# Sliding-window attention followed by a feed-forward pair: loads per pair, a new order of the transfers, first value casts on ScalarE, attention steps spread through the feed-forward, groups of 384 tokens

## The chip, the cores and the metric

One core of a Trainium2 chip. The metric is the device time of one execution in microseconds (us), the median over several runs. Two kernels that are compared ran on the same chip, in turns. A ratio is the mean time of one kernel's fast runs over that of the other's fast runs of the same rounds, so it is not quite the ratio of the medians that are quoted.

The engines are TensorE (PE, with PEld for its weight loads), VectorE (DVE), ScalarE (ACT), GpSimd (POOL) and SyncE (SP), which here only issues DMAs. The clock that the traces record for PE is either full (1.0) or half (0.5).

A line of a timeline reads: start and duration in us, engine, line of the kernel, operation, output<-inputs, shapes, how many instructions are merged in the line; in brackets the idle time in us just before it and what ended it.

## The reference, cut to what matters

```python
# q, k, v: (8 batches, 8 heads, 576 positions, 64); window 32
scores = q @ k.T / 8, masked to |i - j| <= 32
attn = softmax(scores);  x = attn @ v           # reshaped to (4608 tokens, 512)
h = x @ w_in                                     # 512 -> 2048
out = np.maximum(0.01 * h, h) @ w_out            # 2048 -> 512, float32
```

## The kernel before

Attention is cut into 64 steps: 8 batches, 2 halves of 288 queries, 4 pairs of heads. A step scores one pair against its window (`score`), takes exp on ACT, multiplies by a mask on POOL, and then sums and weights the values on PE (`weighted`); DVE takes the reciprocal of the sums and writes the result into `xT`.

```python
def score(i):
    ...  # 5 matmuls into ps (one buffer)
    nc.scalar.activation(out=e, in_=ps[...], func=AF.Exp, scale=scale)
    nc.gpsimd.tensor_mul(pr, e, mask[hf])

def weighted(i):
    ...  # 2 matmuls with ones into s, 5 with vbd into x (one buffer each)
    nc.vector.reciprocal(r, s)
    nc.vector.tensor_mul(xT[:, p, t0:t0 + HALF], x, r)

def step():                      # i = next step
    step_transposes(...)         # of the next batch's q and k, on PE
    score(i + 1)
    weighted(i)
    ...                          # casts of the next batch (POOL), loads of the one after (SP)
```

The feed-forward works on groups of tokens: `h_tile` (4 matmuls, then a leaky ReLU on ACT) and `o_tile` (16 matmuls, a copy on DVE into one of two `o_sb` buffers, a DMA out). All engines run in program order, so where a step stands between the tiles decides what PE can do while the chain of the step runs. The start of the kernel:

```python
for i in range(NPAIR):                       # steps 0 to 3
    score(i + 1)
    if i + 1 < NPAIR:
        cast_v(0, i + 1)                     # POOL
    load_w_in(512 * i, 512 * i + 512)        # issued by POOL
    weighted(i)
...
load_after(1, w_in_bf[0:1, 0, 1024:1026])    # q, k of batch 1, behind the third quarter of w_in
load_v(1, 0, NPAIR)
...  # h of 512 tokens, with steps 4 to 7
...  # w_out issued after the casts of batch 1
for p in range(NPAIR):                       # steps 8 to 11
    if p + 1 < NPAIR:
        cast_v(1, p + 1)
    step()
load_after(2, ...); load_v(2, 0, NPAIR)      # whole loads of batch 2
o_tile(0, 0); o_tile(0, 1); step(); o_tile(256, 0); step(); o_tile(256, 1)

groups = [(512 + 256 * i, 256) for i in range(3)]
groups += [(1280 + 512 * i, 512) for i in range(6)] + [(1280 + 512 * 6, 256)]
...  # chunks: 16 to 32 h matmuls or one o_tile each; before each, as many steps as its deadline asks
```

The softmax here doesn't subtract the row's maximum and nothing guards it: scores larger than these inputs give would overflow.

## Time and profile before

| | before |
|---|---|
| median (4 runs, those of the later comparison) | 389.96 us |
| span of the profiled run | 386.2 us |
| PE busy | 338.7 us (88%) |
| mean granted clock of PE | 0.958 |
| DVE, ACT, POOL busy | 56%, 44%, 47% |
| dense matmul work, worked out in the prediction | 310.9 us |

The row to read is the difference between the span and the dense work: 75.3 us in which PE either waits or runs at half clock. The prediction below shows the lines that this rests on.

### The profile page before, as it was taken

How to read it: one execution, taken by the hardware profiler on the slowest of the kernel's cores; microseconds unless marked ns; L12 is line 12 of the kernel's file. 1: busy time of each engine (PE TensorE's matmuls, PEld its weight loads, DVE VectorE, ACT ScalarE, POOL GpSimd, SP SyncE). 2: the span in 40 equal slices, each digit the busy share in tenths (PEclk: the TensorE clock that was granted, in tenths of full speed). 3: DMA queues.
4: the chain of work that ended last, by engine and by line, in shares of the span. 5: the costliest groups of instructions: out<-in, count | busy, mean ns of one | idle time of the engine just before them, and what ended most of it. 6: DMA issues, size and time to landing. Idle time of an engine off the chain costs nothing.

```text
span 386.2 us, 6261 instructions
## 1 busy us (share of the span) xinstructions
PE 338.7 (88%) x2496; PEld 201.9 (52%) x2496; DVE 215.2 (56%) x242; ACT 171.8 (44%) x325; POOL 182.4 (47%) x216
## 2 busy tenths in 40 slices
PE   2549775984699799999999997999799989999995
PEld 2337563443577567455555554555455545544472
DVE  4575838319567776137866757574748575600201
ACT  5716481023556537373276244723563255045060
POOL 7596798065655756025566528363735332100000
PEclk9999896897899999999999998999989999999999
DMA  8979996994946590920737290929101100110101
GB/s 193 173 111 167 239 185 110 247 171 143 229 52 168 133 145 36 225 76 27 126 80 209 94 176 0 230 72 139 40 0 39 71 2 1 56 54 0 73 38 54
DMA packets 60004, 42.34 MB, mean 110 GB/s; under 512 B 38984, under 2 KB 55368, under 8 KB 59976
## 3 DMA queue, kind: packets, MB, share of 16 engines
q1 hardware_dynamic: 55688, 37.76, 46.0%
q0 software_dynamic: 4288, 4.20, 7.2%
q8 instruction: 19, 0.31, 0.4%
q14 instruction: 9, 0.07, 0.1%
HBM read 36.70 MB, written 9.44 MB: 119 GB/s over the span
## 4 chain that ended last, share of the span: by engine, by line
PE 68%; DVE 3%; ACT 1%; issue 1%; POOL 1%; DVEq 0%; POOLq 0%
PE mm L266 29%; PE mm L257 29%; PE x L239 3%; PE ps L213 3%; PE tp L180 3%; DVE r L245 2%; PE s L231 1%; PE s L232 1%; ACT e L219 1%; DVE xT L247 0%; POOL pr L223 0%; POOL qb L161 0%; DVE o_sb L271 0%; ACT kT L194 0%; DVEq L247 0%
## 5 line engine op out<-in xcount | busy, mean ns | idle before, releaser
L223 POOL TENSOR_TENSOR pr<-e,mask 128x544 bf16<-128x544 bf16 x64 | 77.5, 1212 | 138.4 <-ACT e L219 127.9
L257 PE MATMUL mm<-xT,w_in_bf 128*128 128x256 bf16 (+1 forms) x768 | 138.5, 338 | 2.4 <-DVE xT L247 2.4
L245 DVE RECIPROCAL r<-s 128x288 f32<-128x288 f32 x64 | 125.2, 1957 | 21.8 <-PE s L232 20.7
L261 ACT ACTIVATE gT<-mm 128x256 bf16<-128x256 f32 (+1 forms) x192 | 93.8, 491 | 87.0 <-PE mm L257 82.9
L266 PE MATMUL mm<-w_out_bf,gT 128*128 128x512 bf16 x576 | 130.5, 383 | 0.0
L257 PEld LDWEIGHTS <-w_in_bf 128*128 128x128 bf16 x768 | 76.9, 102 | 53.2 <-issue 6.2
L266 PEld LDWEIGHTS <-gT 128*128 128x128 bf16 x576 | 55.8, 99 | 63.6 <-issue 2.5
L271 DVE COPY o_sb<-mm 128x512 f32<-128x512 f32 x36 | 24.9, 691 | 82.1 <-PE mm L266 72.4
L197 DVE COPY kbd<-kT 64x576 bf16<-64x576 bf16 x64 | 28.6, 447 | 53.3 <-ACT kT L194 52.8
L219 ACT ACTIVATE e<-ps 128x544 bf16<-128x544 f32 x64 | 39.9, 624 | 26.3 <-PE ps L213 26.2
L168 POOL CAST vbd<-vf 64x576 bf16<-64x576 f32 x64 | 42.3, 660 | 2.1 <-DMA vf<-in_v_dram 0.2
L194 ACT ACTIVATE kT<-tp 128x576 bf16<-128x576 bf16 x32 | 20.8, 649 | 49.3 <-PE tp L180 48.3
L188 ACT ACTIVATE qT<-tp 128x576 bf16<-128x576 bf16 x32 | 20.7, 648 | 40.5 <-PE tp L180 40.4
L231 PE MATMUL s<-pr,ones_bd 128*128 128x288 bf16 x64 | 19.8, 309 | 19.2 <-DVE r L245 13.3
L247 DVE TENSOR_TENSOR xT<-x,r 128x288 bf16<-128x288 f32 x64 | 29.3, 458 | 6.7
L239 PE MATMUL x<-pr,vbd 128*128 128x128 bf16 (+2 forms) x320 | 28.4, 225 | 3.1 <-POOL vbd L168 2.2
L213 PE MATMUL ps<-qT,kbd 128*128 128x128 bf16 (+2 forms) x320 | 28.4, 224 | 2.1 <-ACT e L219 1.8
L161 POOL CAST kb<-kf 96x768 bf16<-96x768 f32 x32 | 26.5, 828 | 7.6 <-DMA kf<-in_k_dram 7.6
L239 PEld LDWEIGHTS <-vbd 128*128 128x128 bf16 x320 | 22.3, 104 | 9.2 <-POOL vbd L168 3.7
L180 PE MATMUL tp<-ident,qb 96*128 96x96 bf16 x192 | 15.1, 221 | 11.8 <-DVE qb L161 6.7
L213 PEld LDWEIGHTS <-kbd 128*128 128x128 bf16 x320 | 20.1, 105 | 4.3 <-issue 2.7
L180 PEld LDWEIGHTS <-qb 96*128 96x128 bf16 x192 | 12.6, 106 | 17.1 <-DVE qb L161 9.3
(30 smaller groups left out, 114.4 us busy)
## 6 DMA issues: line engine op xcount, KB each, us to landing
qf<-in_q_dram SPq DMA_DIRECT2D x32, 288.0 KB, 4.3
kf<-in_k_dram SPq DMA_DIRECT2D x32, 288.0 KB, 7.1
out_dram<-o_sb SPq DMA_DIRECT2D x36, 256.0 KB, 2.1
vf<-in_v_dram SPq DMA_DIRECT2D x14, 576.0 KB, 11.2
w_in_bf<-in_moe_w_in_dram POOLq DMA_DIRECT2D x8, 256.0 KB, 4.7
w_out_bf<-in_moe_w_out_dram POOLq DMA_DIRECT2D x4, 512.0 KB, 12.0
vf<-in_v_dram SPq DMA_DIRECT2D x4, 144.0 KB, 6.9
vf<-in_v_dram SPq DMA_DIRECT2D x2, 288.0 KB, 9.2
```

Source lines behind the costliest of these rows:

```text
L168: nc.gpsimd.tensor_copy(out=vbd[b % 2][r, p, :, r], in_=vf[b][r, p])
L180: nc.tensor.transpose(tp[:, c], src[:, p, c].rearrange("p a d -> p (a d)"), ident[0:96, 0:96],)
L197: nc.vector.tensor_copy(out=kbd[b % 2][r, p, :, r], in_=kT[r].rearrange("p (n j) -> p n j", j=64),)
L213: nc.tensor.matmul(ps[:, c0:c0 + n], kbd[b % 2][:, p, blk], qT[b][:, p, q0:q0 + n], start=True, stop=True,)
L219: nc.scalar.activation(out=e, in_=ps[:, 512 - HALF:512 - HALF + NCOL], func=AF.Exp, scale=scale,)
L223: nc.gpsimd.tensor_mul(pr, e, mask[hf])
L239: nc.tensor.matmul(x[:, a:a + n], vbd[b % 2][:, p, blk, :], pr[:, c0:c0 + n], start=(n_ == 0), stop=(n_ == len(WIN[hf]) - 1), skip_group_c ...
L245: nc.vector.reciprocal(r, s)
L247: nc.vector.tensor_mul(xT[:, p, t0:t0 + HALF], x, r)
L257: nc.tensor.matmul(h[:, 0:n], w_in_bf[:, c, ts(f, 128)], xT[:, c, ds(t0, n)], start=(c == 0), stop=(c == DMC - 1),)
L261: nc.scalar.activation(out=gT[t0][:, f, 0:n], in_=h[:, 0:n], func=AF.Prelu, alpha=0.01)
L266: nc.tensor.matmul(o, gT[t0][:, f, ts(j, 128)], w_out_bf[:, f, :], start=(f == 0), stop=(f == FFC - 1),)
```

## The change

Its intent: have every transfer and cast of the start ready earlier, never let attention steps stand alone on PE, and make the deadlines of the steps gentler. The diff, cut to its core:

```diff
-    def load_qk(b, p0, p1): ...     # one tile for all pairs
+    def load_qk(b, p, behind=None): # one tile per pair; `behind` makes it wait for other data
 ...
-            nc.gpsimd.tensor_copy(out=vbd[b % 2][r, p, :, r], in_=vf[b][r, p])
+            if on_act:
+                nc.scalar.activation(out=vbd[...], in_=vf[b, p][r], func=AF.Copy)
+            else:
+                nc.gpsimd.tensor_copy(out=vbd[...], in_=vf[b, p][r])
 ...
-            step_transposes(8 * (b + 1) + PLAN[b > 1][0][r])
+            step_transposes(max(upto - 1, 8 * (b + 1)))
         score(i + 1); weighted(i)
+            step_transposes(upto)    # the last one follows the step
+        # each load follows the cast of its own pair
 ...
     score(0)
+    load_w_in(0, 512)
     first_pair(); ...; cast_qk(0, 3, nc.vector)
+    load_w_in(512, 1024)
     for i in range(NPAIR):
         score(i + 1)
-            cast_v(0, i + 1)
-        load_w_in(512 * i, 512 * i + 512)
+            cast_v(0, i + 1, on_act=True)
+        if i < 2: load_w_in(1024 + 512 * i, 1536 + 512 * i)
+        else: load_w_out(i - 2)
         weighted(i)
 ...
+    # q, k of batch 1 behind the second quarter of w_in; step 4; the rest of w_out
+    # steps 5 to 7 inside the first h group; v of batch 1 behind the second quarter of w_out
 ...
-    for p in range(NPAIR): (cast_v); step()          # steps 8 to 11, then 4 o_tiles with 2 steps
+    for p in range(NPAIR):
+        if p < 3:
+            cast_v(1, p); (at p == 2 also cast_v(1, 3))
+            o_tile(256 * (p // 2), p % 2, step if p == 2 else None)   # one step midway
+            step()
+        else:
+            o_tile(256, 1)
+        load_qk(2, p)
+    for p in range(NPAIR): load_v(2, p)
 ...
-    groups += [(1280 + 512 * i, 512) for i in range(6)] + [...]
+    groups += [(1280 + 384 * i, 384) for i in range(8)] + [...]
-    LEAD, RATE = 2, 1.2
+    RATE = 1.3                       # lead 1 for the first 12 chunks, then 2
```

## The prediction

> **What bounds the kernel now.** I read the page's busy row first, then its slices, then the same core cut into stages, then TensorE's timeline.
>
> ```profile
> span 386.2 us, 6261 instructions
> PE 338.7 (88%) x2496; PEld 201.9 (52%) x2496; DVE 215.2 (56%) x242; ACT 171.8 (44%) x325; POOL 182.4 (47%) x216
> ...
> PEclk9999896897899999999999998999989999999999
> DMA  8979996994946590920737290929101100110101
> ```
>
> TensorE (PE) is the bound: nothing else exceeds 56%. But busy is not full speed: the granted clock falls to 0.6 to 0.8 in some early slices, and the first slices are not full either. The stage table (columns: PE, weight loads, DVE, ACT, POOL busy, clock, DMA share, GB/s) shows where:
>
> ```profile
> 0.00:28.00 28.00, 12.14 (x101) 8.24 (x102) 16.61 (x25) 13.59 (x18) 21.04 (x36) 1.00 0.93 160
> 28.00:54.70 26.70, 23.93 (x222) 18.92 (x220) 16.96 (x20) 16.58 (x42) 21.17 (x21) 0.94 1.13 194
> 54.70:111.10 56.40, 40.16 (x313) 26.27 (x309) 30.92 (x34) 18.74 (x38) 32.78 (x39) 0.82 0.93 175
> 111.10:332.00 220.90, 212.11 (x1603) 122.66 (x1601) 141.83 (x153) 107.18 (x198) 107.38 (x121) 0.98 0.42 93
> ```
>
> I turn this into a budget. Where PE runs dense, the chain of waits gives the pitch of each block: one step of attention 0.24+0.12+0.11+0.24 = 0.71 us, one transposed pair half (six matmuls) 0.26, one output tile (16 matmuls of 512) 3.45, 32 first-layer matmuls of 256 columns 3.49. The whole program is 64 x 0.71 + 64 x 0.26 + 36 x 3.45 + 12 x 3.49 + 384 x 0.2157 (the 512-wide first layer) = 310.9 us. So 386.2 - 310.9 = 75.3 us are lost to idling and to half clock. By stage, span less dense work:
> - 0 to 28.0 (batch 0 until the first h matmul): 28.0 - 5.2 = 22.8
> - 28.0 to 54.7 (h of 512 tokens, steps 4 to 7, transposes of batch 1): 26.7 - 18.8 = 7.9
> - 54.7 to 111.1 (steps 8 to 17, the first four output tiles): 56.4 - 30.4 = 26.0
> - after 111.1: 275.1 - 256.5 = 18.6, of which 8.5 are waits, 3.4 half clock, 3.9 the tail after the last matmul.
>
> The third stage is the worst. TensorE there:
>
> ```profile
> 60.43 0.40 PE L231 MATMUL s<-pr,ones_bd 128*128 128x288 bf16 x1 [1.75 <-POOL pr L223]
> ...
> 63.09 0.42 PE L231 MATMUL s<-pr,ones_bd 128*128 128x288 bf16 x1 [1.15 <-DVE r L245]
> ...
> 65.78 0.42 PE L231 MATMUL s<-pr,ones_bd 128*128 128x288 bf16 x1 [1.06 <-DVE r L245]
> ...
> 66.75 8.97 PE L266 MATMUL mm<-w_out_bf,gT 128*128 128x512 bf16 x32
> ...
> 90.77 0.28 PE L231 MATMUL s<-pr,ones_bd 128*128 128x288 bf16 x1 [3.67 <-DVE r L245]
> ```
>
> Steps 8 to 11 stand alone, with no feed-forward work between them, and each costs about 2.65 us instead of 0.71: the reciprocal (1957 ns) plus xT (458 ns) on DVE set the pitch. PE cools, so the first 32 output matmuls take 8.97 us instead of 6.9. The 3.67 us come from elsewhere, as DVE's timeline shows: its copy of an output tile waited 8.36 us for an output DMA, which SyncE issued only after the whole loads of batch 2.
>
> ```profile
> 87.23 0.69 DVE L271 COPY o_sb<-mm 128x512 f32<-128x512 f32 x1 [8.36 <-DMA out_dram<-o_sb]
> ```
>
> In the first stage POOL sets the pitch, some 3.8 us a step:
>
> ```profile
> 21.19 1.21 POOL L223 TENSOR_TENSOR pr<-e,mask 128x544 bf16<-128x544 bf16 x1
> 22.35 1.38 POOL L168 CAST vbd<-vf 64x576 bf16<-64x576 f32 x2
> 23.67 1.26 POOL L328 DMA_DIRECT2D w_in_bf<-in_moe_w_in_dram  x2
> 25.00 1.21 POOL L223 TENSOR_TENSOR pr<-e,mask 128x544 bf16<-128x544 bf16 x1
> ```
>
> **What the Trainium skill says.** "TensorE: Matmul & The Clock Gate", section "Part 1: The HAM clock gate": idle PE falls to half clock and needs about 3.4 us of sustained work to regain it. The trace agrees: stretches of clock 0.5, and 13 h matmuls in 2.93 us at 29.5 us against 16 in 1.91 later. Same page, "Back-to-back issue gap": N/2.4 + 2.5 ns; here 16 matmuls of 512 at 3.45 us, 216 ns each, agree. I use it for the new width: 384 columns, 162.5 ns (estimate). "DMA: Bandwidth & Descriptors", "Queues, rings and completion order": each engine takes turns between the rows that have work, packet by packet. No trace of before shows it, because weights (POOL's queue) and activations (SyncE's) never overlap for long. The change makes them overlap. Same page, "Specifications": transfers under 512 B are inefficient. The trace agrees: v's 256 B runs move 158 GB/s between 46 and 52 us at a full DMA share, q/k's 1536 B runs 275 GB/s between 38 and 44.
>
> **The change, part by part.**
> 1. First value casts to ACT, weights earlier. POOL's step falls from 1.21+1.38+1.26 to 1.21+1.28 = 2.5 us; DVE needs 1.96+0.46, so about 2.55 us a step. ACT gains six casts of some 0.65 us (its 128x576 copies take 0.648). pr of step 1 is itself delayed, as two weight DMAs are now issued ahead of it (18.4 to 19.7). I get step 1 at 19.7, 2 at 22.3, 3 at 24.8 to 28, 4 at 28 to 30.5; the spread is when v of pair 3 lands, since its packets now take turns with w_in. First h matmul at about 30 instead of 28.0, but with step 4 already done (0.71). Net of that, 1.3 us worse.
> 2. DMA order. At the measured rates batch 0 ends at 18.3; w_in 10.4 us (the 10.8 us of w_out from 52.5 to 63.3, packed), q/k 1 8.9, w_out 10.4, v 1 7.5: if packed, everything is in by about 55 us, against 63.3 before. Taking turns packet by packet I get q/k 1 in at 40, w_out at 49, v 1 at 54. All just in time: output tiles start at 52, the last v is cast at 60.
> 3. Steps 4 to 7 and h of 512 tokens: dense 18.8 - 0.7 = 18.1, plus about 2 us of cold start, 0.5 us for xT of step 7, 1.5 for transposes and ACT: 22 us. h ends at 52 instead of 54.7: **2.7 us gained** (parts 1 to 3 together).
> 4. Steps 8 to 11 between output tiles of 3.45 us (or halves of 1.73), outputs issued ahead of the next loads. PE per step is 4.2 us, DVE's 2.4 + 0.69 = 3.1: hidden. At the half tile, PE 2.4 against DVE 3.1, and POOL has two casts of v in a row (2.76 us) ahead of a pr: 0.7 + 1.2 us remain. The back-to-back transposes' 0.74 us waits (3.0 in total) go too, as the second now follows the step; one is left. With odd waits the loss falls from 26 to about 4: **22 us gained**.
> 5. Groups of 384. Instruction order: before has four places with two steps and no feed-forward block between them (the 2.0 us waits at 132, 238, 278, and 0.9+0.5 at 315); after has three, with transposes between the steps, about 1.7 us each = 5.1, and perhaps one cold window (1.7). Steps now come every 20 h matmuls (3.3 us) or output tile (3.5), so DVE (2.4 + 0.9 for kbd + part of 0.69) fits within 4.2 to 4.5. 128 more matmuls cost 128 x 2.5 ns = 0.3 us. Loss 18.6 to about 13.5: **5 us gained**, less 0.3.
>
> Sum: 2.7 + 22 + 4.7 = 29 us; span 357. Timed runs lie 2 to 4 us above the span (profiled run 388.28 on 386.2, median 389.89), so 360 us.
>
> **Rivals.**
> - The new overlap of queues hurts: v of pairs 2 and 3 land late, ACT (in order) holds exp behind the cast, PE stands still and cold; or w_out is not in at 52 us. For: the DMA share is already about 0.9 to 1.1 up to 60 us, and everything lands just in time. Against: total bytes are unchanged and all of it is in 8 us earlier. This costs 5 to 8 us: 365 to 368.
> - A new wait takes the place of the old: POOL and SyncE work in order, and each load now waits for its pair's cast, so outputs can stick behind a load and block the two o_sb buffers. For: the 8.36 us wait is of that kind. Against: only one pair is held at a time. Losing half of part 4: 370.
> - Smoothing with 384 tokens does nothing since the waits just move: 364.
> - All transfers are early and h starts at 27: 353.
> - The change is hidden altogether (PE is 88% busy): would need the 26 us to reappear elsewhere, and dense work is 311 us. Unlikely.
>
> **Range and chances.** The first two rivals are likelier than the good one, and they stretch the upper side: 351 to 371 in 8 of 10. Faster by over 2% means under 382, which still holds if three quarters of the gain fails: 0.96; within 2% 0.03; slower 0.01.
>
> **What would show it.** In the profile after: the stage of steps 8 to 17 takes about 35 us instead of 56, with clock near 1 from 35 us on; no o_sb copy waiting 8 us for an output DMA; w_in, q/k 1 and w_out moving side by side, DMA full until about 55 us and then falling; first h matmul near 30 us; PE waits after 111 us of some 5 us on the reciprocal, in three places. PE busy should fall to about 325 us although it has 128 more matmuls. I am wrong if a stretch with low clock remains between 55 and 110 us, if PE waits on DMA for w_out or on the value casts by over 3 us, or if the waits after 111 us stay at 8.5.

## The result, and the profile after

The changed kernel takes 355.52 us (median of 4 runs, 355.11 to 355.59) against 389.96; the ratio is 0.911, 95% interval 0.907 to 0.915. Executions over 1.5% slower than the fastest of the same kernel are left out of the means. Span and engines of the profiled run after, then PE's clock and the DMA share by slice:

```profile
span 353.9 us, 6635 instructions
...
PE 324.3 (92%) x2600; PEld 208.2 (59%) x2624; DVE 211.8 (60%) x242; ACT 183.4 (52%) x363; POOL 178.7 (51%) x213
...
PEclk9999999999999999999999999999999999999999
DMA  8999986599995274342453265340010010020101
```

PE is busy for 14 us less although it has 128 more matmuls: from 30 us on, the half clock is gone in every slice. Ahead of that the row can't be trusted, in either kernel: it shows full clock, but the matmuls take half-clock times, as six transposes show, early and later:

```profile
16.86 0.66 PE L187 MATMUL tp<-ident,kb 96*128 96x96 bf16 x6 [0.28 <-POOL kb L165]
...
40.36 0.42 PE L187 MATMUL tp<-ident,qb 96*128 96x96 bf16 x6
```

DMA is nearly full to about 53 us, relaxes, and is nearly full again from 71 to 106 us. The same stages as in the prediction (to the first h matmul; h of 512 tokens and steps 4 to 7; a stretch with as much dense work, 30.5 us, as before's steps 8 to 17 with four output tiles; the rest), columns as there:

```profile
0.00:28.27 28.27, 13.44 (x114) 9.59 (x115) 18.41 (x27) 18.07 (x25) 23.14 (x38) 1.00 1.14 202
28.27:49.46 21.19, 20.20 (x209) 16.88 (x208) 14.97 (x18) 15.99 (x41) 13.28 (x14) 1.00 1.02 229
49.46:82.37 32.91, 31.26 (x258) 20.04 (x259) 21.83 (x24) 14.16 (x31) 23.47 (x28) 1.00 0.85 182
82.37:353.90 271.53, 259.43 (x2028) 161.66 (x2046) 156.57 (x174) 135.15 (x268) 118.85 (x136) 1.00 0.36 95
```

The third stage has fallen from 56.40 to 32.91 us. PE there, where steps 8 to 11 now have output tiles around them:

```profile
53.40 0.29 PE L238 MATMUL s<-pr,ones_bd 128*128 128x288 bf16 x1
...
54.14 0.41 PE L246 MATMUL x<-pr,vbd 128*128 128x96 bf16 x5 [0.34 <-POOL vbd L175]
54.38 3.62 PE L273 MATMUL mm<-w_out_bf,gT 128*128 128x512 bf16 x16
...
58.08 0.29 PE L238 MATMUL s<-pr,ones_bd 128*128 128x288 bf16 x1
...
61.70 0.41 PE L246 MATMUL x<-pr,vbd 128*128 128x96 bf16 x5 [0.64 <-POOL vbd L175]
...
64.44 0.28 PE L238 MATMUL s<-pr,ones_bd 128*128 128x288 bf16 x1 [0.36 <-POOL pr L230]
```

Where before had waits of 1.0 to 1.8 us at each step, there are now 0.34, 0.64 and 0.36 us at three of the four, and the tile takes 3.62 us, at full clock. At the start POOL no longer casts values between a mask product and a weight load:

```profile
19.14 1.26 POOL L336 DMA_DIRECT2D w_in_bf<-in_moe_w_in_dram  x2
20.41 1.23 POOL L230 TENSOR_TENSOR pr<-e,mask 128x544 bf16<-128x544 bf16 x1
21.57 1.27 POOL L336 DMA_DIRECT2D w_in_bf<-in_moe_w_in_dram  x2
22.84 1.23 POOL L230 TENSOR_TENSOR pr<-e,mask 128x544 bf16<-128x544 bf16 x1
```

The pitch of POOL is 2.43 us instead of 3.8, and DVE takes over as the limit: PE's steps 1 to 4 start at 19.27, 21.93, 24.61 and 27.30, 2.68 apart, and the last three wait for the reciprocal, as here:

```profile
21.93 0.42 PE L238 MATMUL s<-pr,ones_bd 128*128 128x288 bf16 x1 [1.15 <-DVE r L252]
```

**A ledger of lost time.** To see where each part acts, I take the start of the row-sum matmul of step k and subtract the dense work of all matmuls ahead of it in program order (N/2.4 + 2.5 ns each, summing to 310.9 us before and 311.2 after). What is left is what PE has lost until then. The last row is the span less all dense work.

| lost us until | before | after | steps bunched | groups 512 | casts POOL | old order | before + spread | even steps |
|---|---|---|---|---|---|---|---|---|
| step 4 | 25.6 | 21.9 | 22.6 | 22.9 | 25.4 | 21.3 | 26.5 | 22.2 |
| step 8 | 33.6 | 25.7 | 29.0 | 26.9 | 29.8 | 37.2 | 41.2 | 26.4 |
| step 12 | 41.8 | 27.7 | 39.3 | 29.5 | 31.5 | 40.2 | 44.7 | 28.0 |
| step 18 | 56.9 | 29.2 | 40.8 | 44.9 | 33.0 | 41.7 | 60.1 | 29.6 |
| step 44 | 64.2 | 38.2 | 49.7 | 50.4 | 42.0 | 50.6 | 70.8 | 31.2 |
| end | 75.3 | 42.7 | 54.2 | 58.3 | 46.5 | 55.2 | 80.2 | 35.3 |

The first two columns: of the 32.6 us won, 3.7 are won up to step 4, another 4.2 up to step 8, 6.2 between steps 8 and 12, 13.6 between 12 and 18, and 4.9 later. The other columns belong to the experiments. Single entries wander by about 1 us from run to run (the loss at step 0 lay between 12.0 and 13.4 us over all runs), so differences under that are not read.

### The profile page after: what moved, and what is told of

Read it like the earlier page. It is cut to its first block, busy times and chain, and to the rows that moved or that the text cites. A ratio compares the mean times of both kernels' runs of the same rounds, so it can differ in the third digit from the quotient of the medians.

```text
span 353.9 us, 6635 instructions
## 1 busy us (share of the span) xinstructions
PE 324.3 (92%) x2600; PEld 208.2 (59%) x2624; DVE 211.8 (60%) x242; ACT 183.4 (52%) x363; POOL 178.7 (51%) x213
## 3 DMA queue, kind: packets, MB, share of 16 engines
q1 hardware_dynamic: 56388, 37.76, 42.7%
## 4 chain that ended last, share of the span: by engine, by line
PE 77%; DMA 7%; DVE 6%; POOL 4%; SPq 2%; issue 2%; ACT 1%; DVEq 0%; POOLq 0%; ACTq 0%
PE mm L273 33%; PE mm L264 31%; DMA kf<-in_k_dram 7%; DVE r L252 5%; PE x L246 3%; PE tp L187 3%; PE ps L220 3%; PE s L238 2%; PE s L239 2%; SPq L71 1%; POOL vbd L175 1%; POOL vbd L400 1%; SPq L82 1%; DVE xT L254 1%; POOL pr L230 1%
## 5 line engine op out<-in xcount | busy, mean ns | idle before, releaser
L252 DVE RECIPROCAL r<-s 128x288 f32<-128x288 f32 x64 | 125.1, 1954 | 38.5 <-PE s L239 38.2
L264 PE MATMUL mm<-xT,w_in_bf 128*128 128x384 bf16 (+1 forms) x896 | 132.7, 304 | 0.9 <-ACT kT L201 0.8
L268 ACT ACTIVATE gT<-mm 128x384 bf16<-128x384 f32 (+1 forms) x224 | 99.0, 445 | 63.0 <-PE mm L264 58.6
L273 PE MATMUL mm<-w_out_bf,gT 128*128 128x512 bf16 x552 | 126.8, 379 | 1.3
L264 PEld LDWEIGHTS <-w_in_bf 128*128 128x128 bf16 x896 | 86.6, 98 | 38.0 <-issue 1.3
L175 POOL CAST vbd<-vf 64x576 bf16<-64x576 f32 x58 | 38.3, 661 | 1.9
L246 PE MATMUL x<-pr,vbd 128*128 128x128 bf16 (+2 forms) x320 | 26.9, 217 | 2.0 <-POOL vbd L175 1.0
L220 PE MATMUL ps<-qT,kbd 128*128 128x128 bf16 (+2 forms) x320 | 27.3, 219 | 0.3
L220 PEld LDWEIGHTS <-kbd 128*128 128x128 bf16 x320 | 21.1, 102 | 8.1 <-issue 0.6
L246 PEld LDWEIGHTS <-vbd 128*128 128x128 bf16 x320 | 21.4, 101 | 7.1 <-issue 2.8
L165 POOL CAST qb<-qf 96x768 bf16<-96x768 f32 x24 | 19.7, 820 | 0.0
## 6 DMA issues: line engine op xcount, KB each, us to landing
w_out_bf<-in_moe_w_out_dram POOLq DMA_DIRECT2D x4, 512.0 KB, 13.5
```

Source lines behind the costliest of these rows:

```text
L165: eng.tensor_copy(out=dst[:, p], in_=src[b, p].rearrange("p a (c d) -> p c a d", d=D),)
L175: nc.gpsimd.tensor_copy(out=vbd[b % 2][r, p, :, r], in_=vf[b, p][r])
L220: nc.tensor.matmul(ps[:, c0:c0 + n], kbd[b % 2][:, p, blk], qT[b][:, p, q0:q0 + n], start=True, stop=True,)
L246: nc.tensor.matmul(x[:, a:a + n], vbd[b % 2][:, p, blk, :], pr[:, c0:c0 + n], start=(n_ == 0), stop=(n_ == len(WIN[hf]) - 1), skip_group_c ...
L264: nc.tensor.matmul(h[:, 0:n], w_in_bf[:, c, ts(f, 128)], xT[:, c, ds(t0, n)], start=(c == 0), stop=(c == DMC - 1),)
L268: nc.scalar.activation(out=gT[t0][:, f, 0:n], in_=h[:, 0:n], func=AF.Prelu, alpha=0.01)
```

## The experiments

Times of the variants are to be compared with 355.52 us (changed kernel) or with the kernel before, which ran beside each of them at medians of 388.94 to 390.32. They ran on two chips (experiments 1 to 4, 8, 9 and the last edit of 10 on one, 5, 6, 7 and the even steps of 10 on the other), and the kernel before differs between these by 1.4 us. A difference of under some 2 us from 355.52 is thus not clear of noise.

### 1. Steps bunched again

```diff
+    cast_v(1, 0)
     for p in range(NPAIR):
+        if p + 1 < NPAIR: cast_v(1, p + 1)
+        step()
+    for p in range(NPAIR):
-        (cast_v; o_tile with step inside; step)
+        o_tile(256 * (p // 2), p % 2)
         load_qk(2, p)
```

> The changed kernel, but steps 8 to 11 stand together ahead of the four output tiles, as they did before; transfers, casts and groups stay as changed. Theory (spreading these steps took most of the 23.6 us that the stage lost less): each bunched step costs about 2.65 us instead of 0.71, the first one also waits some 2 us for its exp and mask, and TensorE falls to half clock for a window or two, so 8 to 11 us are given back: 363.5 to 366.5 us, with 0.5 clock between 50 and 65 us and reciprocal waits of 1 to 2 us in each of the four steps. Rival (the gain came from earlier transfers and from outputs that no longer queue behind loads): 355.5 to 357.5 us.

Measured: 366.06 us (365.15 to 367.09), ratio to before 0.940. PE of this run:

```profile
57.26 0.40 PE L238 MATMUL s<-pr,ones_bd 128*128 128x288 bf16 x1 [2.03 <-POOL pr L230]
...
59.92 0.42 PE L238 MATMUL s<-pr,ones_bd 128*128 128x288 bf16 x1 [1.15 <-DVE r L252]
...
62.61 0.42 PE L238 MATMUL s<-pr,ones_bd 128*128 128x288 bf16 x1 [1.06 <-DVE r L252]
...
64.42 5.92 PE L273 MATMUL mm<-w_out_bf,gT 128*128 128x512 bf16 x17 [0.22 <-issue]
```

The waits are those of the kernel before, and 17 output matmuls take 5.92 us where 16 take 3.62 above: PE is at half clock for most of them. 10.5 us are given back. The ledger puts 8.3 of them between steps 8 and 12, and 2.6 between steps 4 and 8, where the first bunched step waits for its exp and its mask product (1.32 and 0.95 us). The theory holds: spreading these four steps is worth 10.5 us in the changed kernel. But 10.5 is not 22.

### 2. Loads of batch 2 ahead of the first outputs

```diff
+    for p in range(NPAIR): load_qk(2, p)
     for p in range(NPAIR):
         if p < 3:
             cast_v(1, p)
+            load_v(2, p)           # and load_v(2, 3) at p == 2
             o_tile(...); step()
-        load_qk(2, p)
-    for p in range(NPAIR): load_v(2, p)
```

> The changed kernel, but SyncE issues the loads of batch 2 ahead of the first output tiles instead of between them (q and k of all pairs first, each v right after its cast). The steps stay spread. Theory (spreading carried the stage; the output copy that waited 8.4 us was a smaller part): 0 to 4 us lost, 355.5 to 359.5 us, the copy of an output tile waits a few us for an output DMA. Rival (the stuck outputs were the main part of the 26 us): 8 us or more lost, 363 us or more.

Measured: 357.47 us (356.86 to 357.60), 2.0 us more, ratio to before 0.917, interval 0.913 to 0.922. That interval overlaps the one of the changed kernel (0.907 to 0.915), so the size of the loss is not clear of noise. DVE of this run:

```profile
68.01 0.69 DVE L280 COPY o_sb<-mm 128x512 f32<-128x512 f32 x1 [3.69 <-DMA out_dram<-o_sb]
```

The output copy is stuck again, for 3.69 us, and the reciprocal behind it on DVE is late; PE loses only about 1.2 us on it. The mechanism is there in the trace, and it is small.

### 3. Groups of 512 tokens with the old pacing

```diff
-    groups += [(1280 + 384 * i, 384) for i in range(8)] + [...]
+    groups += [(1280 + 512 * i, 512) for i in range(6)] + [...]
-    RATE = 1.3 ; lead = 1 if cj < 12 else 2
+    RATE = 1.2 ; lead = 2
```

> The changed kernel with the old groups of 512 tokens and the old pacing of the steps. Theory (smaller groups give later deadlines, so fewer double steps): the 3.9 us come back, 358 to 361 us, with reciprocal waits of 2.0 us again in three or four places after 110 us and half clock after some. Rival (the deadlines only move, the waits are the same): 355 to 356.5 us.

Measured: 370.24 us (369.25 to 371.49), ratio to before 0.951. 14.7 us lost, four times what I expected, so the theory had the size wrong. The ledger shows where: 15.4 us between steps 12 and 18, against 1.5 in the changed kernel, and hardly any difference after step 18 (13.4 against 13.5), where the theory had put it. The first group of 512 needs 28 steps done by the 13th chunk, that of 384 only 24, so the rule asks for four steps in front of the first chunk. This variant is a little harsher than the kernel before, which came to that point with 14 steps done instead of 12.

### 4. First value casts back on POOL

```diff
-            cast_v(0, i + 1, on_act=True)
+            cast_v(0, i + 1)
```

> The changed kernel with the first value casts back on POOL. Theory (POOL's 3.9 us set the pitch of the first steps): three steps take 3.9 instead of 2.69 us, so the first h matmul is at 31 to 32 instead of 28.3 us, and 3 to 4 us are lost: 358.5 to 359.5 us. Rival (the first stage is bound by the transfers, and a later stage has slack that takes up the delay): 355.5 to 357 us.

Measured: 358.96 us (357.66 to 360.47), 3.4 us lost; PE's steps 1 to 4 start at 19.82, 23.62, 27.43 and 30.79, 3.4 to 3.8 us apart, waiting on POOL for the mask product and then for the cast:

```profile
23.62 0.40 PE L238 MATMUL s<-pr,ones_bd 128*128 128x288 bf16 x1 [1.39 <-POOL pr L230]
...
24.95 0.63 PE L246 MATMUL x<-pr,vbd 128*128 128x96 bf16 x5 [0.72 <-POOL vbd L175]
```

The first h matmul is at 31.65 us. The ledger keeps the 3.5 us it loses by step 4 to the end (46.5 against 42.7). The theory holds; no slack behind takes it up.

### 5. The old order of the transfers in the changed kernel

```diff
-    load_w_in(0, 512) ... load_w_in(512, 1024)     # early
     for i in range(NPAIR):
-        (w_in quarters 3, 4, then w_out quarters 1, 2)
+        load_w_in(512 * i, 512 * i + 512)
 ...
+    load_v(1, ...)                                 # right after q, k of batch 1
     # after the casts of q, k of batch 1:
-    load_v(1, ...) behind w_out
+    load_w_out(0 to 3)
```

> The changed kernel with the old order of the transfers: w_in issued one quarter per step from step 0 on, q/k 1 behind the third quarter, v 1 next, w_out last and only after the casts of q/k 1. Steps stay spread, groups stay 384. Theory (the new order is what lets output tiles run at 50 us; spreading depends on it): w_out lands at 60 to 63 us, TensorE waits for it at the first output tile some 8 to 11 us and cools, 365 to 369 us. Rival (the order is worth only what the h stage gained): 357 to 361 us.

Measured: 367.45 us (366.40 to 369.08), ratio to before 0.944: 11.9 us lost. PE at the first output tile:

```profile
51.37 1.89 PE L273 MATMUL mm<-w_out_bf,gT 128*128 128x512 bf16 x4 [2.50 <-DMA w_out_bf<-in_moe_w_out_dram]
56.82 1.87 PE L273 MATMUL mm<-w_out_bf,gT 128*128 128x512 bf16 x4 [3.57 <-DMA w_out_bf<-in_moe_w_out_dram]
...
62.71 1.87 PE L273 MATMUL mm<-w_out_bf,gT 128*128 128x512 bf16 x4 [1.23 <-DMA w_out_bf<-in_moe_w_out_dram]
```

Four waits of 8.2 us in all, and four matmuls in 1.87 us are at half clock. The ledger has 37.2 instead of 25.7 at step 8 and no further difference. So the order pays by letting the first output tile run at 50 us.

### 6. Spreading alone, on the kernel before

```diff
-    for p in range(NPAIR): (cast_v); step()
     load_after(2, ...)
-    load_v(2, 0, NPAIR)
-    o_tile(0, 0); o_tile(0, 1); step(); o_tile(256, 0); step(); o_tile(256, 1)
+    for p in range(NPAIR):
+        (cast_v; at p == 2 load_v(2, 0, NPAIR))
+        o_tile(256 * (p // 2), p % 2, step if p >= 2 else None)
+        step()
```

> The kernel before with one part of the change: steps 8 to 13 between and inside the first four output tiles, loads of batch 2 issued ahead of them. Theory: the first output tile has to wait for w_out until about 64 us, so about half of the 23.6 us is won: 374 to 380 us. Rival (spreading does nothing without the new order, since the outputs queue behind the loads of batch 2): 386 to 391 us.

Measured: 390.23 us (388.86 to 393.05), ratio to before 1.003, interval 0.997 to 1.010: nothing. The rival's number, mostly by another way than it gave. PE, and DVE ahead of its last wait:

```profile
59.42 1.89 PE L266 MATMUL mm<-w_out_bf,gT 128*128 128x512 bf16 x4 [3.19 <-DMA w_out_bf<-in_moe_w_out_dram]
...
83.87 0.30 PE L231 MATMUL s<-pr,ones_bd 128*128 128x288 bf16 x1 [2.88 <-DVE r L245]
```

```profile
81.25 0.69 DVE L273 COPY o_sb<-mm 128x512 f32<-128x512 f32 x1 [2.68 <-DMA out_dram<-o_sb]
```

Between steps 8 and 12 it loses 3.5 us instead of 8.2, so spreading works; but ahead of step 8 it has lost 7.6 us more, at the wait for w_out and the half clock that goes with it. The rival's own way takes part too: most of the 3.5 us is the wait of 2.88 us at 83.87, for a reciprocal behind an output copy that waited for an output DMA. Steps 12 to 18 cost 15.4 us as before (15.1). Spreading needs the order of the transfers, and it does nothing for steps 12 to 18.

### 7. Groups of 384 alone, on the kernel before

The same edit of groups, chunks and pacing as in the change, applied to the kernel before.

> The kernel before with groups of 384 tokens and the new pacing alone. Theory (this part works by itself after 110 us): 3 to 5 us faster, 385 to 387 us. Rival (it also packs more steps early, where the casts of q, k and v on POOL and late loads cannot keep up): 388 to 393 us.

Measured: 372.55 us (369.70 to 375.37; one of the four runs is slow, the profiled one); ratio of fast runs 0.954, interval 0.946 to 0.962. With that alone the kernel before gains 4.6%, some 18 us, about four times what I expected. The trace is of the slow run, so I read only the coarse part: the four bunched steps 8 to 11 are still there with their waits of 1.06 to 1.15 us, past step 18 it loses 9.3 us (before: 18.4), and between steps 12 and 18 it still loses 9.5 us (before: 15.1), where an output copy again waits 8.7 us for an output DMA. So here the size gives back only part of what is lost between steps 12 and 18.

### 8. Size or pacing? Groups of 512 with the new rule, groups of 384 with the old one

> The changed kernel with groups of 512 tokens but the new pacing rule. Computed from the two rules, steps ahead of the first 13 blocks after step 11: 3 2 1 1 2 1 1 2 1 1 0 0 0 here, 4 2 1 1 1 1 2 1 1 1 0 0 0 with the old rule (measured 370.2 us), 1 1 1 1 1 1 1 2 1 1 2 1 1 in the changed kernel. Theory (the size sets the deadlines: the first group of 512 needs 28 steps where that of 384 needs 24, and the loss comes where steps 12 to 17 crowd): 362 to 367 us, lost between steps 12 and 18. Rival (the pacing rule made the difference): 356 to 358 us.

> The changed kernel with groups of 384 tokens but the old pacing rule; steps ahead of the first 13 blocks: 2 1 1 1 1 1 1 2 1 1 1 1 2. Theory (the size matters, not the rule): 355 to 358 us. Rival: 363 us or more.

Measured: 366.40 us (365.76 to 366.76) with 512 and the new rule, 356.85 (356.14 to 357.04) with 384 and the old one. The size makes the difference, 10.9 us; the rule's 1.3 are not clear of noise. The old rule with 384 moves losses rather than adding any: 5.5 us between steps 12 and 18 (changed kernel: 1.5), but 10.2 after step 18 (13.5). (For the 11th block with 512 the expectation lists no step; by the rules, and in the trace at 133.43 us, there is one. Nothing rests on it.) PE with groups of 512 and the new rule:

```profile
71.95 0.43 PE L187 MATMUL tp<-ident,qb 96*128 96x96 bf16 x6 [2.36 <-POOL qb L165]
...
75.69 0.66 PE L187 MATMUL tp<-ident,qb 96*128 96x96 bf16 x6 [1.95 <-POOL qb L165]
...
84.85 0.41 PE L187 MATMUL tp<-ident,qb 96*128 96x96 bf16 x6 [0.79 <-ACT kT L201]
```

Crowded steps do not only wait for their own chain: the transposes between them wait for the casts of the next batch on POOL, which come one step earlier in program order (2.36 and 1.95 us). At 75.69 six transposes take 0.66 us instead of 0.42: half clock once more. The ledger of this run: 28.1 at step 12, 38.9 at step 18, 54.2 at the end.

### 9. All transposes ahead of the step again

```diff
-            step_transposes(max(upto - 1, 8 * (b + 1)))
+            step_transposes(upto)
```

> The changed kernel with all transposes of a step ahead of it again, as before. In steps 13 to 15 both halves of a pair then follow each other through one PSUM buffer, and the second waits 0.74 us for ACT's copy of the first. Theory (these waits are all that this part removed): 3 x 0.74 = 2.2 us lost, 357 to 358.5 us. Rival (hidden behind the chain of the step, which sets the pace anyway): 355.5 to 356.5 us.

Measured: 358.20 us (357.71 to 358.97), 2.7 us lost. PE's waits for ACT's copy of a transposed q, in total, times and longest, first in this run, then in the changed kernel:

```profile
PE tp L187 <- ACT qT L195: 4.0, 7, 0.8
```

```profile
PE tp L187 <- ACT qT L195: 2.2, 3, 0.7
```

Four more waits, 1.8 us. Four of this run's stand at 75, 81, 86 and 92 us, 0.74 to 0.76 us each; there the ledger loses 3.7 us between steps 12 and 18, against 1.5. Waits for POOL and for the reciprocal trade places as well (6.2 and 3.3 us in total here, 1.6 and 7.0 in the changed kernel). From step 12 to the end the ledger gives 16.9 us against 15.0, so 1.9 us belong to this part; the rest was lost ahead of step 12 and is close to what the start wanders by. As expected, a little small.

### 10. A version with evenly laid out steps

What the changed kernel still waits for after 82 us (total, times, longest):

```profile
PE s L238 <- DVE r L252: 3.8, 5, 1.2
PE tp L187 <- ACT qT L195: 2.2, 3, 0.7
PE x L246 <- DVE xT L254: 0.8, 5, 0.2
```

All but one of these waits follow from two steps that have no feed-forward block between them, at 103, 120, 136, 202 and 218 us. The rule in the kernel makes them: it takes as many steps as the deadlines ask, all ahead of one chunk. I laid the steps out by hand:

```diff
-    for ci, ...: goal = ...; while state["done"] < min(goal, NC): step()
+    skip = (11, 16, 20, 36, 42)                # chunks without a step ahead
+    inside = {10: 11, 11: 5, 15: 11, 16: 5}    # a step after so many matmuls of this output tile
+    for ci, ...: one step ahead of each chunk that is not skipped
```

> The changed kernel with the steps after 69 us laid out by hand: one per block of 16 output or 20 to 24 first-layer matmuls, three steps over two output tiles where one more is needed, five blocks left without, no two steps adjacent. Theory (what is left after 82 us, 6.8 us of waits of which 6 follow from adjacent steps, is TensorE waiting on the chain of one step): 5 to 6 us faster than the changed kernel, 349.5 to 350.5 us. Rival (DVE or POOL, which have under 1 us of slack per step, make the waits reappear at the denser places): 353 to 355.5 us.

Measured: 348.69 us (347.75 to 349.44), ratio to before 0.895, interval 0.891 to 0.900. Waits after 82 us:

```profile
PE tp L187 <- ACT qT L195: 0.7, 1, 0.7
PE s L238 <- DVE r L252: 0.3, 1, 0.3
PE x L246 <- DVE xT L254: 0.2, 1, 0.2
```

6.8 us of waits became 1.2, and the time fell by 6.8 (by the ratios to the kernel before, some 6): it beats both kernels, by as much as expected or a little more. DVE and POOL had the slack. From step 18 to the end this version loses 5.7 us, of which about 4 lie behind the last matmuls.

One more edit on top, q/k of batch 1 behind the first quarter of w_in:

> The version with evenly laid out steps (348.7 us), and q/k of batch 1 issued behind the first instead of the second quarter of w_in. They share the engines with w_in some 2 to 3 us longer. Theory (q/k of pair 3 came last and cost 0.8 us of waiting ahead of the last transposes): 347 to 348.5 us. Rival (w_in's last quarters come later and the h matmuls wait for them): 349 to 352 us.

Measured: 347.94 us (347.75 to 348.71, 6 runs). Ratios to before are 0.894 and 0.895 for the two versions, with overlapping intervals: inconclusive, though the rival (a loss) is not seen.

## Why the prediction was right, and where it was not

The time was predicted at 360.0, range 351 to 371; it is 355.5. The sum was right; one step of it was right in total and wrong in what it was put down to.

- **Part 1, casts and first steps.** Predicted for steps 1 to 4: 19.7, 22.3, 24.8 to 28, 28 to 30.5. Measured: 19.27, 21.93, 24.61, 27.30, so a little ahead of the early end of each range. The feared lateness of v did not come: ACT never waited for a v load. Counted in the trace, v's packets of 256 B end at 18 us, and the first ones of the weights move at 17: the two hardly shared the engines. "1.3 us worse" was thus wrong by its sign: in its own terms (the first h matmul at 28.27, step 4 done) the stage is 0.4 us better, and in the ledger the loss by step 4, some h matmuls included, is 3.7 us smaller. Experiment 4 gives the casts 3.4 us.
- **Part 2, order.** The queues do take turns packet by packet: between 32 and 44 us, counted in the trace, each 2 us moved 211 to 218 packets of w_out (1024 B) and 196 to 209 of q and k (1536 B). w_in was not among them, against the prediction: it had landed by 29.9. w_out was in time for the first output tile, as predicted. q/k of batch 1 came in at 46.7, not 40. The one-element DMA that gates them was issued at 22.77 and the loads behind it only at 27.39, a delay of 4.6 us that the prediction did not have; whether it is the whole reason is not shown. The lateness cost one wait of 0.76 us. The order as a whole is worth 11.9 us (experiment 5), which I had not given it: it is the condition for part 4.
- **Part 3.** h ends at 49.5, predicted 52, for the reason in part 1 and because the clock was already full from about 30 us on.
- **Part 4, the step that failed.** "With odd waits the loss falls from 26 to about 4: 22 us gained", put down to steps 8 to 11 between output tiles and outputs ahead of loads. The stage did lose only 2.4 us (32.91 less 30.5 of dense work). But that total agrees in part by luck: I had cut the sum by stages of time and named one part of the change for each stage. The ledger and experiments 1, 3, 6 and 8 show that in this window the spreading acts on steps 8 to 12, and that the larger share, 13.6 us between steps 12 and 18, in the changed kernel depends on the size of the groups: with 512 tokens most of it is lost again (15.4 and 10.8 us in the two variants), and spreading alone leaves it where it was. In the kernel before, the size alone wins only some 5.6 of its 15.1 us there (experiment 7, a slow run's trace), and the output copy that the prediction named still waits there for 8.7 us. So both are needed, and 13.6 us is not the share of one of them.
- **Part 5.** "5 us gained" for groups of 384: after step 18 it is 4.9, but that agreement is luck too. The mechanism was fewer double steps; there are five instead of three (before had four), at 1.6 to 2.2 us each by the ledger, of which 1.1 to 1.4 are waits. What is better is that none costs as much as before's worst (up to 4.8) and that no half clock follows them. And the size did not win it: with groups of 512 in the changed kernel the loss after step 18 is 13.4 us (old rule) or 15.3 (new rule), against 13.5; with all transposes ahead of the step it is 13.2. Which part won these 4.9 us stays open; no run undoes the loads per pair in the later batches. The real worth of the groups is 10.9 us for the size and 14.7 with the pacing, because the deadline of the first large group reaches back to 70 us. The estimate of 162.5 ns for a matmul of 384 columns held: at 218.94 us, 19 of them take 3.25 us, the last one 0.33, so 162 ns from one to the next.
- **The end of the sum.** The timed run lies 1.6 us above the span, not 3. With 2.5 us at the start, 1.6 in the third stage and 0.9 the other way in the last, that is the 4.5 us between 360.0 and 355.5 (to 0.1).

The rivals: the overlap of the queues did not hurt; outputs stuck behind loads are worth some 2 us, not clear of noise (experiment 2); that 384 only moves the waits is refuted by experiments 3, 7 and 8.

The values of undoing single parts (10.5, 2.0, 14.7, 3.4, 11.9, 2.7) sum to 45.2 us, more than the 34.4 that the change gained. They are not shares: parts depend on each other, as 5 and 6 show, where spreading is worth 10.5 us with the new order and nothing without it. What stays open is how much of the 10.8 us in experiment 8 is waiting on casts and how much half clock; no run took these apart. The trace gives a first cut: between steps 12 and 18 PE waited 4.3 us for POOL's casts and 1.5 for ACT's copies, and the rest, some 5 us, goes to the half clock (mean clock 0.82 there) and to short gaps.

## What to carry to other kernels

Cut a budget by parts of the change, not only by stages of time: a scheduling constant late in the program (here the size of a group) can act through its deadlines on a stage far ahead, and reading the instruction order for how many steps stand in front of each block shows that in advance. Where one engine is the bound and a chain over others is longer than its own share of a step, lay such steps out one per block of independent work, by hand if a rule would pile them up; and check that the data of the block is there, or the spreading only trades one wait for another.

## What the Trainium skill lacked or had wrong

- "TensorE: Matmul & The Clock Gate", section "Why this matters for your kernels", advises to avoid idle gaps of over some 3 us. In the kernel before, a wait of 2.02 us, with one of 0.26 us some 3 us ahead of it, was followed by half clock, at 238 us and again at 278. PE's wait and, for the stretch around it, all engines with the clock 0.89:

```profile
238.51 0.42 PE L231 MATMUL s<-pr,ones_bd 128*128 128x288 bf16 x1 [2.02 <-DVE r L245]
```

```profile
230.00:240.00 10.00, 7.62 (x71) 4.70 (x68) 6.55 (x7) 6.23 (x11) 6.63 (x8) 0.89 0.15 50
```

  A like wait at 132 us was not followed by it, and none of the waits of up to 1.24 us after 82 us in the changed kernel was. But with groups of 512 and the new rule (experiment 8) the clock was at half for most of 86 to 90 us (mean 0.60), and no wait in the 8 us ahead was longer than 0.79 us. So a gap under 3 us is not safe in itself; what divides the cases is not shown.
- "DMA: Bandwidth & Descriptors" has no figure for how long a tiny DMA takes on busy engines. The one-element load that holds q/k of batch 1 back took 4.6 us from its issue to the next issue (22.77 to 27.39), and 4.5 in the last version, with w_in running. The second one, for v of batch 1, took 7.6 us (38.24 to 45.84), with q and k ahead of it on the same queue. As a gate it is not free.
